# First-layer products of two MLPs over pairs of blocks, halves and chunks (seven products for eight), with softplus in place

## Chip, cores and metric

One core of one Trainium2 chip. The metric is the device time of one execution in microseconds; lower is better. Given are the median of three runs and one profiled execution.

## The reference

Forgetting attention, then two MLPs with 512 model and 2048 hidden columns on 2304 tokens (4 batches, 8 heads, 576 positions, 64 columns a head):

```python
scores = scale * np.matmul(q, k.transpose(0, 1, 3, 2))
decay = cum[:, :, :, None] - cum[:, :, None, :]        # cum: running sum of log f
scores = np.where(causal, -1000000000.0, scores + decay)
...
x = attn_out.transpose(0, 2, 1, 3).reshape(B * S, H * D)
h = x @ w_in1;  g = np.maximum(h, 0.0) + alpha * np.minimum(h, 0.0);  x = g @ w_out1
h = x @ w_in2;  g = np.maximum(h, 0.0) + np.log1p(np.exp(-np.abs(h)));  out = g @ w_out2
```

All is float32 except the MLP weights, which come as float64 (the kernel gets them as 64-bit words).

## The kernel before, in words

**Precision.** Every MLP operand is kept as two parts, a high part (a cast on ScalarE) and a low part (the rest, by a subtraction), and each product is three matmuls: low weight by high data, high by low, high by high. TensorE is PE in the rows, VectorE DVE, ScalarE ACT, GpSimd POOL, and SP issues the DMAs.

**Tiling.** Tokens are cut into 6 chunks of 384 (`CH`), hidden columns into 16 blocks of 128 (`NFF`) in 4 groups of 4 (`G`). `hidden` makes one block for one chunk: 12 matmuls of 384 columns (L889: three part products by four 128-row slices of the model), then the activation. In the first MLP that is two Relu on ScalarE (L896, L899) and a combination on VectorE (L902); in the second VectorE takes −|h| (L911), ScalarE softplus (L915), and VectorE adds max(h, 0) (L918). L925 casts the high part of g, L928 makes the low part. `product` adds four blocks of a group into a bank `o` (L946: 48 matmuls of 384 columns in the first MLP for a chunk's four outputs, of 512 in the second for three), `total` adds that to an accumulator (L965 for the first group, L967), and makes the parts of the second MLP's input (L975, L978) or stores (L982).

**Weights.** `weights` loads a block's raw words and turns them into two parts: on ScalarE L394 and L413, on VectorE L397, L401, L405, L409, L416 and L420. For the first MLP the parts are also stored to DRAM (`w_d`) and loaded again for a second use (L372).

**Stages.** 16 pairs of heads make attention (lines L508 to L804), the first eight with nearly all memory to themselves. Then `switch1` gives half of attention's extra memory to the MLP, and the first MLP for chunks 0 to 2 (`NA` = 3) runs as filler between the attention products of the last eight pairs. Attention rows of the last two batches go to DRAM split into parts (`xb_d`, L811, L814) and are fetched after attention (`fetch`, L849). `switch2` then hands out the rest of the memory, and the first MLP for chunks 3 to 5 and the whole second MLP follow.

**What sets the order.** `Plan` collects every operation with its engine, a length, what it reads and writes, and a rank; `emit` plays it through as a list schedule over buffer slots and writes out each engine's instructions in the order found. The ranks are built from the numbers in `TUNE`. On the chip each engine then works its list strictly in that order.

## Time and profile before

| | us |
|---|---|
| median of 3 runs (1036.82 to 1041.52) | 1039.47 |
| span of the profiled execution, first to last instruction | 1035.1 |
| TensorE busy in it | 1022.3 |
| VectorE busy | 725.1 |
| ScalarE busy | 518.5 |
| GpSimd busy | 240.3 |

The time of the profiled execution as a whole isn't recorded apart from its span; the median lies 4.4 us above the span. Matmuls are pipelined, so a matmul's duration in a row is longer than the step from one to the next, and a busy TensorE isn't by itself TensorE at its peak. Idle time of an engine that nothing waits for costs nothing.

### The profile page before, as it was taken

The page shows a single profiled execution, that of the slowest core. Times are in us where ns is not written, and L with a number is a line of the kernel's source. Part 1 is how long each engine was busy: PE and PEld are TensorE (multiplying, and loading weights), DVE is VectorE, ACT ScalarE, POOL GpSimd, SP SyncE. Part 2 cuts the span into 40 slices and gives each one's busy share as a digit, 9 for nine tenths or more (in the row PEclk, how much of TensorE's full clock was granted, in tenths as well). Part 3 has the DMA queues.
Part 4 walks back from the last instruction along what each step waited for, and adds up shares of the span by engine and source line. Part 5 has one row for each costly group of instructions (what it writes and reads, how often), then busy time and mean ns, then how long its engine had stood idle before and what let it go on. Part 6 is the DMA issues. An engine that isn't in the chain of part 4 may idle for free.

```text
span 1035.1 us, 17156 instructions
## 1 busy us (share of the span) xinstructions
PE 1022.3 (99%) x6023; PEld 946.4 (91%) x6023; DVE 725.1 (70%) x1605; ACT 518.5 (50%) x1264; POOL 240.3 (23%) x399
## 2 busy tenths in 40 slices
PE   8899999999999999999999999999999999999998
PEld 6678899999999899999999999999999998999997
DVE  5898789979999988532335488738765885685543
ACT  6778777776767655344333354434522332332221
POOL 7677766355566520000000000000000000000000
PEclk8999999999999999999999999999999999999999
DMA  7676446646654248020412221202110211010102
GB/s 185 158 225 176 106 124 198 196 147 184 198 167 144 92 159 288 18 71 32 142 40 84 82 61 34 69 1 82 39 45 1 82 41 42 1 41 1 61 31 91
DMA packets 114021, 101.94 MB, mean 98 GB/s; under 512 B 66624, under 2 KB 87248, under 8 KB 113936
## 3 DMA queue, kind: packets, MB, share of 16 engines
q1 hardware_dynamic: 113936, 100.86, 32.3%
q8 instruction: 47, 0.77, 0.3%
q14 instruction: 38, 0.31, 0.1%
HBM read 78.66 MB, written 22.17 MB: 97 GB/s over the span
## 4 chain that ended last, share of the span: by engine, by line
PE 81%; DVE 7%; ACT 4%; issue 3%; POOL 3%; DMA 2%; POOLq 0%; ACTq 0%; DVEq 0%; SPq 0%
PE o L946 36%; PE h L889 35%; PE pt L725 3%; PE pt L621 3%; PE pt L660 2%; POOL d L599 2%; ACT p L651 1%; PE pt L508 1%; DVE d L643 1%; DMA raw<-in_moe_w_in_dram 1%; PE pt L634 1%; DVE p01l L685 1%; DVE ca L409 1%; DVE g L928 1%; DVE acc L967 1%
## 5 line engine op out<-in xcount | busy, mean ns | idle before, releaser
L946 PE MATMUL o<-g,wout 128*128 128x384 f32 x1152 | 213.6, 337 | 0.0
L946 PE MATMUL o<-wout,g 128*128 128x512 f32 x864 | 205.2, 391 | 0.0
L946 PEld LDWEIGHTS o<-g,wout 128*128 128x128 f32 x1152 | 199.4, 188 | 2.3 <-issue 1.9
L946 PEld LDWEIGHTS o<-wout,g 128*128 128x128 f32 x864 | 161.5, 188 | 32.0
L925 ACT CAST g<-h 128x384 fp32r<-128x384 f32 x192 | 92.2, 481 | 141.4 <-PE o L946 126.7
L928 DVE TENSOR_TENSOR g<-h,g 128x384 fp32r<-128x384 f32 x192 | 106.2, 554 | 80.6 <-ACT g L925 79.8
L599 POOL TENSOR_SCALAR d<-cumb,cumc 64x576 f32<-64x576 f32 (+4 forms) x160 | 117.8, 740 | 96.2 <-ACT p L651 90.9
L915 ACT ACTIVATE ta<-ta 128x384 f32<-128x384 f32 x96 | 50.4, 525 | 135.5 <-DVE ta L911 135.2
L902 DVE SCALAR_TENSOR_TENSOR h<-ta,slope,h 128x384 f32<-128x384 f32 x96 | 58.9, 613 | 73.6 <-ACT h L899 73.4
L651 ACT ACTIVATE p<-d,mx 128x128 f32<-128x128 f32 (+2 forms) x144 | 84.4, 588 | 25.8 <-DVE mx L643 24.8
L896 ACT ACTIVATE ta<-h 128x384 f32<-128x384 f32 x96 | 47.3, 492 | 95.2 <-PE h L889 94.6
L911 DVE TENSOR_SCALAR ta<-h 128x384 uint32<-128x384 uint32 x96 | 53.3, 555 | 39.5 <-PE h L889 39.5
L918 DVE SCALAR_TENSOR_TENSOR h<-h,ta 128x384 f32<-128x384 f32 x96 | 54.2, 564 | 38.1 <-ACT ta L915 37.9
L643 DVE CUSTOM_DVE_ANT_0 d<-pt,d 128x128 f32<-128x128 f32 (+2 forms) x144 | 65.3, 477 | 9.7 <-PE pt L626 4.6
L967 DVE TENSOR_TENSOR acc<-o,acc 128x512 f32<-128x512 f32 (+1 forms) x102 | 60.3, 621 | 16.8 <-PE o L946 16.6
L660 PE MATMUL pt<-ident,p 128*128 128x128 f32 (+1 forms) x400 | 65.1, 281 | 4.7 <-ACT p L651 4.3
L660 PEld LDWEIGHTS pt<-ident,p 128*128 128x128 f32 (+1 forms) x400 | 45.7, 140 | 12.3 <-ACT p L651 7.8
L889 PE MATMUL h<-x1h,win 128*128 128x384 f32 x256 | 54.8, 339 | 0.9 <-DVE g L928 0.9
L889 PE MATMUL h<-x2h,win 128*128 128x384 f32 x256 | 55.3, 340 | 0.1
L394 ACT ACTIVATE ca<-raw 128x512 f32<-128x512 f32 x64 | 43.1, 675 | 24.3 <-DMA raw<-in_moe_w_in_dram 11.6
L889 PE MATMUL h<-x0h,win 128*128 128x384 f32 x256 | 54.9, 339 | 0.3 <-DVE g L928 0.3
L889 PE MATMUL h<-x5h,win 128*128 128x384 f32 x256 | 53.5, 335 | 0.0
(157 smaller groups left out, 1909.8 us busy)
## 6 DMA issues: line engine op xcount, KB each, us to landing
raw<-in_moe_w_in_dram SPq DMA_DIRECT2D x32, 512.0 KB, 3.7
raw<-in_moe_w_out_dram SPq DMA_DIRECT2D x32, 512.0 KB, 3.7
cumb<-cum_d SPq DMA_DIRECT2D x30, 288.0 KB, 4.5
out_dram<-acc SPq DMA_DIRECT2D x18, 256.0 KB, 2.1
...
```

The source lines that it names most:

```text
L599: nc.gpsimd.tensor_scalar(out=buf(dk)[r, 0:w], in0=buf(cb)[r, hh, 0:w], scalar1=-1.0, scalar2=cumc[r, e, i:i + 1], op0=ALU.mult, op1=ALU.add,)
L643: nc.vector.tensor_tensor_reduce(out=d[:, c0:c1], in0=buf(key)[:, 0:c1 - c0], in1=d[:, c0:c1], scale=-1.0, scalar=least, op0=ALU.add, op1= ...
L651: nc.scalar.activation(out=buf(pk)[:, 0:w], in_=buf(dk)[:, 0:w], func=AF.Exp, bias=buf(mk)[:, x:x + 1], scale=-1.0, accum_out=buf(sm)[:, e ...
L660: nc.tensor.transpose(out=buf(tk[x])[0:rows, (j - j0) * 128:(j - j0) * 128 + 128], in_=buf(pk)[:, j * 128:j * 128 + rows], identity=ident,)
L889: nc.tensor.matmul(out=hb(), lhsT=w_[:, kk * 128:kk * 128 + 128], rhs=x_[:, kk, :], start=(s == 0), stop=(s == len(ops) - 1))
L902: nc.vector.scalar_tensor_tensor(out=hb(), in0=buf(ka), scalar=slope[:, ff:ff + 1], in1=hb(), op0=ALU.mult, op1=ALU.add)
L911: nc.vector.tensor_scalar(out=buf(ka).bitcast(U32), in0=hb().bitcast(U32), scalar1=0x80000000, scalar2=None, op0=ALU.bitwise_or)
L918: nc.vector.scalar_tensor_tensor(out=hb(), in0=hb(), scalar=0.0, in1=buf(ka), op0=ALU.max, op1=ALU.add)
L925: nc.scalar.copy(out=buf(kg)[0], in_=hb())
L928: nc.vector.tensor_sub(buf(kg)[1], hb(), buf(kg)[0].bitcast(F32))
L946: nc.tensor.matmul(out=buf(ok)[:, 0:width], lhsT=a, rhs=b_, start=(j == 0 and s == 0), stop=(j == G - 1 and s == 2))
L967: nc.vector.tensor_add(buf(ok)[:, 0:width] if inner else ac(), buf(ok)[:, 0:width], ac())
```

## The change

Only chunks 0 and 1 (`NA` = 2) keep the old way beside attention. The other work is cut into five sweeps (`SWEEPS`): first MLP for chunk pairs (2, 3) and (4, 5), second MLP for all three pairs. In a sweep eight half-steps (`inner`) each take two hidden blocks by two chunks, with the 512 model columns in two halves. That is a 2-by-2 product of 2-by-2, and it is made by Strassen's seven products in Winograd's form (`FORM`) instead of eight: 42 matmuls (L1095) instead of 48. The products need sums of weight blocks (`first_weights`: 4 sums and 7 low parts on L1023, GpSimd except for the first two half-steps; 7 casts on L1043, ScalarE) and sums of chunks and halves (`sources`: 4 subtractions on L983, 7 casts on L990, 7 low parts on L993; VectorE for the first sweep, GpSimd for 3 low parts and the subtractions of the others). Their results are put together in PSUM: a copy on ScalarE (L1108) and five additions on VectorE (L1103) a half-step, before the activation (`bend`). `outer` makes the second products as before, now for each output over a whole group (L902).

Softplus is taken in place in PSUM (L862), without the two VectorE operations around it. A weight's float64 words are first put together to float32 (L391, L395, L399) and then split (L412, L415); the second MLP's are prepared in the first two sweeps (`second_weights`). First-layer weights are stored whole, second-layer weights in parts (`w1_d`, `w2_d`), and each sweep loads them again (L1028, L1069). Attention rows of chunks 2 to 5 go to DRAM whole (`xf_d`, L823) and come back by L963; the first MLP's result goes through DRAM for all chunks (`x1_d`). A third switch gives the early MLP's memory to the sweeps. The numbers in `TUNE` are new.

```diff
-    NA = NC // 2
+    NA = 2
...
-            nc.scalar.mul(out=buf(ua), in_=parts()[1], mul=2.0 ** -112)
+            nc.scalar.activation(out=buf(key), in_=halves()[1], func=AF.Prelu, scale=2.0 ** -112, alpha=-(2.0 ** 32))
...
+            w = buf(key).bitcast(U32)
+            nc.vector.tensor_scalar(out=w, in0=w, scalar1=3, scalar2=None, op0=ALU.logical_shift_left)
...
+        def fill():
+            w = buf(key).bitcast(U32)
+            nc.vector.scalar_tensor_tensor(out=w, in0=halves()[0], scalar=29, in1=w, op0=ALU.logical_shift_right,
+                                           op1=ALU.bitwise_or)
...
+            if c < NA:
+                plan.add("act", t_act(n), hi, reads=[yk], writes=[("X", c, hp, b)], rank=R(n0))
+                plan.add("pool", t_pool2(n), lo, reads=[yk], writes=[("X", c, hp, b)], rank=R(n0))
+            else:
+                plan.add("sp", 0.5, put, reads=[yk], writes=[("xf", c, hp, b)], rank=R(n0), late=0.5)
...
+            def soft():
+                nc.scalar.activation(out=hb(), in_=hb(), func=AF.Softplus)
+            plan.add("act", t_act(CH, sbuf=False), soft, writes=[hk], rank=rank)
...
+    PAIRS = tuple((2 * x, 2 * x + 1) for x in range(NC // 2))
+    SWEEPS = ((0, 1), (0, 2), (1, 0), (1, 1), (1, 2))
+    HALVES = NFF // 2
+    PERIOD = 15.6
...
+    FORM = ((0, 0, 1), (4, 4, 2), (5, 5, 3), (3, 3, 4), (1, 1, 1), (6, 2, 4), (2, 6, 5))
...
+        step = PERIOD / 7 * PACE
+        side = "dve" if s == 0 else "pool"
+        both(0, b11, k11, "dve", first)
+        sub(b11, b12, b11, k11, k12, k11, side, first)
+        sub(tf, b22, b11, tk, k22, k11, side, first + step)
+        both(4, tf, tk, "dve", first + step)
+        sub(b12, b22, b12, k12, k22, k12, side, first + 2 * step)
+        both(5, b12, k12, "dve", first + 2 * step)
+        both(3, b11, k11, "dve", first + 3 * step)
+        both(1, b21, k21, side, first + 4 * step)
+        both(2, b22, k22, side, first + 5 * step)
+        sub(b21, tf, b21, k21, tk, k21, side, first + 6 * step)
+        both(6, b21, k21, side, first + 6 * step)
...
+        side = "dve" if s == 0 and a < 2 else "pool"
...
+        both(0, a11, [src[0]], rank)
+        sum_(0, s1, a21, a22, False, [src[1]])
+        sum_(1, s2, s1, a11, True, [src[0], ("sum", s, a, 0)])
+        both(4, s2, [sk, ("sum", s, a, 1)], rank)
+        sum_(2, s3, a11, a21, True, src)
+        both(5, s3, [sk, ("sum", s, a, 2)], rank)
+        both(3, s1, [sk, ("sum", s, a, 0)], rank)
+        both(1, a12, [src[0]], rank)
+        sum_(3, s4, a12, s2, True, [src[0], ("sum", s, a, 1)])
+        both(6, s4, [sk, ("sum", s, a, 3)], rank)
+        both(2, a22, [src[1]], rank)
...
+        def mult(x):
+            wa, xb, n = FORM[x]
+            wkey, xkey = ("ws", s, a, wa), ("xo", s, xb)
+            def pe():
+                w, (xh, xl) = buf(wkey), buf(xkey)
+                done = n in (1, 4) and first[n] == x
+                ops = [(w[:, c], x_, kk) for c, x_ in ((1, xh), (0, xl), (0, xh)) for kk in range(2)]
+                for i, (w_, x_, kk) in enumerate(ops):
+                    nc.tensor.matmul(out=hb(n), lhsT=w_[:, kk * 128:kk * 128 + 128], rhs=x_[:, kk, :],
+                                     start=(i == 0 and first[n] == x), stop=(i == 5),
+                                     skip_group_check=n in (1, 4))
...
+        mult(0)
+        plan.add("act", t_act(CH, sbuf=False), lambda: nc.scalar.copy(out=buf(p1), in_=hb(1)), reads=[bank[1]], writes=[p1],
+                 rank=at[0])
+        mult(1)
+        add(t[1], h[2], t[0], u2, [bank[2], p1], at[1])
+        mult(2)
+        add(t[2], h[3], t[1], u3, [bank[3], u2], at[2])
+        mult(3)
+        add(h[3], h[4], t[2], bank[3], [bank[4], u3], at[3])
+        mult(4)
+        mult(5)
+        add(h[4], h[4], t[1], bank[4], [u2], at[5])
+        mult(6)
+        add(h[5], t[2], h[5], bank[5], [u3], at[6], True)
+        for n, x, ci, k in ((3, 1, 1, 3), (1, 0, 0, 4), (4, 0, 1, 5), (5, 1, 0, 6)):
+            bend(m, 2 * a + x, bank[n], ("g", s, 2 * a + x, ci), at[k])
...
+            slots(pool, "xo", range(1, 7), [128, 2, CH], F32R, 2)
+            slots(pool, "ws", range(1, 8), [128, 2, 256], F32R)
+            slots(pool, "sf", [0], [128, 4, 256])
+            slots(pool, "g", [7], [128, CH], F32R, 2)
+            slots(pool, "w32", [3], [128, 512])
+            slots(pool, "t", range(4), [128, CH])
+            slots(ps, "h", range(2, 5), [128, 512])
+            slots(ps, "o", [2], [128, 512])
...
+                    first_weights(s, a)
+                    if s < 2:
+                        for kind, ff in spare[2 * (s * HALVES + a):2 * (s * HALVES + a) + 2]:
+                            second_weights(kind, ff, T(s, a))
+                    if a % 2 == 0:
+                        for ff in range(2 * a, 2 * a + 4):
+                            last_weights(s, ff, T(s, a + 1) - 4 * PACE)
+                    inner(s, a)
+                if a >= 2 or s > 0:
+                    s0, g = (s, a // 2 - 1) if a >= 2 else (s - 1, NG - 1)
+                    ne = KD if SWEEPS[s0][0] == 0 else CH // 128
+                    for e in range(ne):
+                        outer(s0, g, a % 2, e, T(s, a + (e + 0.5) / ne))
```

How the instructions move, at three places.

TensorE in the first MLP after attention, before: one block `h` for chunk 4, four model slices at a time, then the next block (`win` are the weight parts, 1 low, 0 high).

```order
L889 MATMUL h_0_1998<-x4h,win_1_100 128x384 x4
L889 MATMUL h_0_1998<-x4l,win_0_99 128x384 x4
L889 MATMUL h_0_1998<-x4h,win_0_99 128x384 x4
L889 MATMUL h_0_4991<-x4h,win_1_92 128x384 x4
L889 MATMUL h_0_4991<-x4l,win_0_91 128x384 x4
L889 MATMUL h_0_4991<-x4h,win_0_91 128x384 x4
```

The same engine now, in the first sweep: products of summed weights `ws` and summed sources `xo` (0 high, 1 low), two slices at a time.

```order
L1095 MATMUL h_0_4704<-xo_0_2009,ws_0_4694 128x384 x2
L1095 MATMUL h_0_4704<-xo_1_2010,ws_0_4694 128x384 x2
L1095 MATMUL h_0_4704<-xo_0_2009,ws_0_4694 128x384 x2
L1095 MATMUL h_0_2012<-xo_0_4677,ws_0_4695 128x384 x2
L1095 MATMUL h_0_2012<-xo_1_4678,ws_0_4695 128x384 x2
L1095 MATMUL h_0_2012<-xo_0_4677,ws_0_4695 128x384 x2
L1095 MATMUL h_0_2013<-xo_0_4679,ws_0_4886 128x384 x2
L1095 MATMUL h_0_2013<-xo_1_4680,ws_0_4886 128x384 x2
L1095 MATMUL h_0_2013<-xo_0_4679,ws_0_4886 128x384 x2
```

A block for one chunk had 12 matmuls of its own; now a bank `h` takes 6 for each product, and four results come out of seven such products.

VectorE right behind attention's last operation, before: accumulations and the finishing of early blocks (`acc`, `g`).

```order
L967 TENSOR_TENSOR acc_1982<-o_0_2000,acc_1982 128x384
L967 TENSOR_TENSOR acc_1982<-o_0_1999,acc_1982 128x384
L967 TENSOR_TENSOR acc_1982<-o_0_2000,acc_1982 128x384
L928 TENSOR_TENSOR g_1_1988<-h_0_1997,g_0_1987 128x384
L416 TENSOR_SCALAR cu_0_90<-cu_0_90 128x512
```

VectorE right behind attention's last operation now: behind three accumulations come weight sums (`sf`), their low parts (`ws`) and the sources' low parts (`xo`), between the early blocks' finishing.

```order
L915 TENSOR_TENSOR acc_103<-o_0_2015,acc_103 128x384
L915 TENSOR_TENSOR acc_103<-o_0_2014,acc_103 128x384
L915 TENSOR_TENSOR acc_103<-o_0_2015,acc_103 128x384
L1023 TENSOR_TENSOR sf_0_4696<-w_0_95 128x256
L1023 TENSOR_TENSOR sf_0_4696<-sf_0_4696,w_0_93 128x256
L993 TENSOR_TENSOR xo_1_4678<-tf_0_2008,xo_0_4677 128x768
L993 TENSOR_TENSOR xo_1_4680<-acc_0_2007,xo_0_4679 128x768
L853 SCALAR_TENSOR_TENSOR h_0_2013<-ta_0_2006,slope,h_0_2013 128x384
L1023 TENSOR_TENSOR ws_0_4689<-sf_0_4696,ws_0_4689 128x256
L1023 TENSOR_TENSOR sf_0_4696<-w_0_93,w_0_95 128x256
L993 TENSOR_TENSOR xo_1_4682<-acc_0_2007,xo_0_4681 128x768
L870 TENSOR_TENSOR g_1_1998<-h_0_2013,g_0_1997 128x384
```

The preparation of the first sweep was moved here, ahead of the first additions that its products wait for.

TensorE at the end of the program, before: the last block's parts of three outputs `o` in turn, so that all three banks end together.

```order
L946 MATMUL o_0_4994<-wout_1_1977,g_0_1993 128x512
L946 MATMUL o_0_4994<-wout_0_1976,g_1_1994 128x512
L946 MATMUL o_0_4994<-wout_0_1976,g_0_1993 128x512
L946 MATMUL o_0_1999<-wout_1_1977,g_0_1993 128x512
L946 MATMUL o_0_1999<-wout_0_1976,g_1_1994 128x512
L946 MATMUL o_0_1999<-wout_0_1976,g_0_1993 128x512
L946 MATMUL o_0_2000<-wout_1_1977,g_0_1993 128x512
L946 MATMUL o_0_2000<-wout_0_1976,g_1_1994 128x512
L946 MATMUL o_0_2000<-wout_0_1976,g_0_1993 128x512
```

TensorE at the end now: the last of the seven products, and behind it the first of six outputs, over four blocks; the last block `g_0_1991` comes from that product.

```order
L1095 MATMUL h_0_4704<-xo_0_4881,ws_0_4691 128x384 x2
L1095 MATMUL h_0_4704<-xo_1_4882,ws_0_4691 128x384 x2
L1095 MATMUL h_0_4704<-xo_0_4881,ws_0_4691 128x384 x2
L902 MATMUL o_0_2015<-wout_1_1982,g_0_4697 128x512
L902 MATMUL o_0_2015<-wout_0_1981,g_1_4698 128x512
L902 MATMUL o_0_2015<-wout_0_1981,g_0_4697 128x512
...
L902 MATMUL o_0_2015<-wout_1_1986,g_0_1991 128x512
L902 MATMUL o_0_2015<-wout_0_1985,g_1_1992 128x512
L902 MATMUL o_0_2015<-wout_0_1985,g_0_1991 128x512
```

Each output is now finished before the next begins, and the first one's last three matmuls need the block that was made last.

## Rows read from the trace of the kernel before

**Rows 1.** Page, part 1: busy us (share of the span) and instructions.
```profile
PE 1022.3 (99%) x6023; PEld 946.4 (91%) x6023; DVE 725.1 (70%) x1605; ACT 518.5 (50%) x1264; POOL 240.3 (23%) x399
```

**Rows 2.** Busy time by stretches (us): total, busy (count) by engine, clock, DMA, GB/s.
```profile
0.00:5.00 5.00, 3.59 (x17) 3.60 (x18) 3.17 (x10) 1.97 (x2) 3.87 (x19) 1.00 0.44 101
9.00:15.00 6.00, 4.96 (x23) 3.38 (x23) 1.61 (x8) 2.46 (x10) 4.95 (x10) 0.50 0.74 199
137.00:260.00 123.00, 121.90 (x793) 114.27 (x793) 111.91 (x264) 91.44 (x239) 68.48 (x111) 1.00 0.60 177
260.00:379.00 119.00, 117.86 (x775) 109.47 (x774) 113.01 (x269) 84.85 (x220) 66.59 (x103) 1.00 0.48 148
379.00:1030.00 651.00, 650.90 (x3474) 615.19 (x3473) 389.65 (x741) 240.95 (x493) 2.86 (x2) 1.00 0.19 61
500.00:600.00 100.00, 100.00 (x579) 100.00 (x578) 44.05 (x84) 34.32 (x77) 0.00 (x0) 1.00 0.24 75
```

**Rows 3.** Chain that ended last, by line: from 379 us, then 260 to 379 us.
```profile
by line: PE o L946 48.7%; PE h L889 47.7%; DMA raw<-in_moe_w_in_dram 0.7%; DVE acc L967 0.6%; DVE g L928 0.3%; DVE ta L911 0.2%; DVE cu L401 0.2%; DVE ca L409 0.2%; DVE cu L416 0.2%; DVE h L918 0.1%; issue 0.1%; DVE cu L397 0.1%; DVE wout L
...
by line: PE h L889 15.5%; PE o L946 14.5%; issue 13.6%; POOL d L599 9.7%; PE pt L725 6.0%; PE pt L621 5.0%; PE pt L660 4.5%; DMA cumb<-cum_d 3.9%; POOL d L609 3.6%; DVE p01l L685 2.3%; DVE d L643 2.1%; DVE cu L401 1.7%; POOL v L579 1.6%; DV
```

**Rows 4.** Line L725 from 375 us: count, ns min/median/max, first and last start.
```profile
L725 PE MATMUL pt<-p01l,v x10: 274/307/309, 375.9 to 378.2; 128*128 128x320 f32 x6, 128*128 128x192 f32 x2, 128*128 128x64 f32 x2
```

**Rows 5.** GpSimd groups by shape: busy us, mean ns | idle before.
```profile
L834 POOL TENSOR_TENSOR x1l<-x,x1h 128x192 fp32r<-128x192 f32 x8 | 4.7, 593 | 1.6 <-ACT x1h L831 1.5
...
L834 POOL TENSOR_TENSOR x2l<-x,x2h 128x384 fp32r<-128x384 f32 x4 | 4.0, 1008 | 0.0
```

**Rows 6.** VectorE groups by shape, same columns.
```profile
L928 DVE TENSOR_TENSOR g<-h,g 128x384 fp32r<-128x384 f32 x192 | 106.2, 554 | 80.6 <-ACT g L925 79.8
...
L902 DVE SCALAR_TENSOR_TENSOR h<-ta,slope,h 128x384 f32<-128x384 f32 x96 | 58.9, 613 | 73.6 <-ACT h L899 73.4
...
L409 DVE SCALAR_TENSOR_TENSOR ca<-ca,raw 128x512 f32<-128x512 uint32 x64 | 46.9, 734 | 0.6
...
L401 DVE SCALAR_TENSOR_TENSOR cu<-raw,cu 128x512 uint32<-128x512 uint32 x64 | 44.7, 698 | 0.5
...
L405 DVE TENSOR_SCALAR ca<-raw 128x512 uint32<-128x512 uint32 x64 | 30.8, 481 | 0.1
...
L397 DVE TENSOR_SCALAR cu<-ca 128x512 uint32<-128x512 uint32 x64 | 28.9, 456 | 4.0 <-ACT ca L394 3.6
...
L416 DVE TENSOR_SCALAR cu<-cu 128x512 uint32<-128x512 uint32 x64 | 28.1, 439 | 4.2 <-ACT win L413 3.7
...
L420 DVE SCALAR_TENSOR_TENSOR wout<-ca,cu 128x512 fp32r<-128x512 f32 x32 | 22.3, 699 | 0.5
...
L685 DVE TENSOR_TENSOR p00l<-pt,p00h 128x256 fp32r<-128x256 f32 x24 | 9.8, 416 | 3.3 <-ACT p00h L681 3.0
```

**Rows 7.** ScalarE groups by shape, same columns.
```profile
L925 ACT CAST g<-h 128x384 fp32r<-128x384 f32 x192 | 92.2, 481 | 141.4 <-PE o L946 126.7 <-DVE h L902 12.3 <-PE h L889 1.0
```

**Rows 8.** DMA issues (median us to landing), and the rate in 40 slices.
```profile
wout<-w_dh SPq DMA_DIRECT2D x12, 256.0 KB, 2.5
...
GB/s 185 158 225 176 106 124 198 196 147 184 198 167 144 92 159 288 18 71 32 142 40 84 82 61 34 69 1 82 39 45 1 82 41 42 1 41 1 61 31 91
```

**Rows 9.** Instructions in order of time at the end: start us, us, what.
```profile
1020.65 10.59 PE L946 MATMUL o<-wout,g 128*128 128x512 f32 x46
...
1029.92 2.05 DVE L967 TENSOR_TENSOR acc<-o,acc 128x512 f32<-128x512 f32 x3 [6.11 <-PE o L946]
```

**Rows 10.** Lines L409, L928 in 150:375 (GpSimd working), then 400:1030 (idle).
```profile
L409 DVE SCALAR_TENSOR_TENSOR ca<-ca,raw x23: 673/690/1753, 152.2 to 370.9; 128x512 f32<-128x512 uint32 x23
...
L928 DVE TENSOR_TENSOR g<-h,g x35: 535/551/560, 151.5 to 373.0; 128x384 fp32r<-128x384 f32 x35
...
L409 DVE SCALAR_TENSOR_TENSOR ca<-ca,raw x32: 681/686/698, 400.1 to 921.4; 128x512 f32<-128x512 uint32 x32
...
L928 DVE TENSOR_TENSOR g<-h,g x150: 547/557/561, 408.2 to 1019.6; 128x384 fp32r<-128x384 f32 x150
```

More of the change, by code (lines that the diff above doesn't have):

```diff
@@ L76, in add, with touch @@
         return n
+    def touch(self, n, key):
+        deps = self.ops[n][3]
+        deps.update(x for x in self.writers.get(key, ()) if x != n)
+        self.readers.setdefault(key, []).append(n)
     def everything(self):
@@ L359, in forgetting_attention_two_mlps, with raw_weights, halves @@
     PT = []
[L362 to L378 removed]
+    def raw_weights(m, kind, ff, rank):
+        key = ("w32", "raw", m, kind, ff)
+        rkey = ("raw", key)
+        def halves():
             words = buf(rkey).bitcast(U32).rearrange("p (n two) -> p n two", two=2)
[L380 to L381 removed]
+            return words[:, :, 0], words[:, :, 1].bitcast(F32)
         def load():
@@ L431, in weights @@
-        plan.add("dve", t_dve(512), low, reads=[ua, uu], writes=[key], rank=rank, port=True)
-        if m == 0:
-            kept.add((kind, ff))
-            if ff < NFF - G:
-                def save():
-                    for a in range(2):
-                        nc.sync.dma_start(out=w_d[a][kind, ff], in_=buf(key)[a].bitcast(F32))
-                plan.add("sp", 1.3, save, reads=[key], writes=[saved], rank=rank, late=2.92)
+            w = buf(key).bitcast(U32)
+            nc.vector.tensor_scalar(out=w, in0=w, scalar1=3, scalar2=None, op0=ALU.logical_shift_left)
@@ new lines, in keep, with save, early_weights @@
+    def keep(m, kind, ff, key, rank):
+        def save():
+            if kind == 0:
+                nc.sync.dma_start(out=w1_d[m][ff], in_=buf(key))
+            else:
+                for a in range(2):
+                    nc.sync.dma_start(out=w2_d[m][ff, :, a], in_=buf(key)[a].bitcast(F32))
+        plan.add("sp", 0.65 * (1 + kind), save, reads=[key], writes=[("wd", m, kind, ff)], rank=rank, late=0.73 * (1 + kind))
+    def early_weights(kind, ff, key, rank):
+        src = raw_weights(0, kind, ff, rank)
+        if kind == 0:
+            keep(0, 0, ff, src, rank)
+        split(key, src, "dve", rank)
+        if kind == 1:
+            keep(0, 1, ff, key, rank)
@@ L990, in output @@
[L990 to L1002 removed]
+                nc.vector.tensor_add(acc(), buf(ok)[:, 0:width], acc())
```

411 lines of the change are left out of this document (219 added, 192 removed), and 3 rows, old and new, of the table TUNE.

## The prediction

> **What bounds the kernel now.** I read the engines' totals first, then the busy time by stretches, then the chain of waits. TensorE is busy for 99% of the span [rows 1], but a busy share doesn't say where it is at its peak, so look at the stretches [rows 2]. From 379 us to 1030 us TensorE is busy 650.9 of 651 us at granted clock 1.00, VectorE 389.7, ScalarE 241, GpSimd 3. There the chain of waits is all products: 48.7% on L946 and 47.7% on L889 [rows 3]. So after attention only fewer or shorter matmuls help. What one costs is its cadence, not its duration in the table, which overlaps the next: 579 matmuls of 384 columns in 500 to 600 us make 172.7 ns each. The order lists 3480 matmuls after attention, 864 of them with 512 columns; (651 − 2616 × 0.1727) / 864 = 230 ns for one of those. Attention's last product starts at 378.2 us [rows 4]. Before that TensorE is still busy 121.9 of 123 and 117.9 of 119 us, but here VectorE is nearly full too (111.9 and 113.0), and the chain from 260 us on names GpSimd, issue and DMA beside TensorE [rows 2, 3]: a mixed stage.
>
> **Matmuls removed: −41.4 us.** In the five sweeps (chunk pairs 1 and 2 of the first MLP, all three of the second) one half-step makes two blocks for two chunks. Before, that was 2 × 2 × 12 = 48 matmuls; now seven products of 6, 42. Five sweeps of 8 half-steps save 240, and the order agrees: 384 + 1680 first-product matmuls where there were 2304; L902 issues the same 2016 as L946 did. 240 × 0.1727 = 41.4 us, on the path, since TensorE had 0.1 us idle there. The shapes (128x128 by 384) don't change, so I keep the cadence.
>
> **What pays for it.** A half-step with its share of second products takes TensorE (42 + 48) × 0.1727 = 15.5 us (second MLP: 42 × 0.1727 + 36 × 0.230, also 15.5). Beside it stand, all new:
> - GpSimd: 4 sums and 7 low parts of 256 columns. The nearest rows are 192 columns 0.593 us and 384 columns 1.008 [rows 5]; on their line 256 costs 0.73 and 768 costs 1.83. So 11 × 0.73 = 8.0, plus 7 source operations of 768 in a sweep, 12.8 / 8 = 1.6: 9.6 of 15.5 us.
> - VectorE: 5 recombining additions at 0.554, 4 low parts at 0.554, in the first MLP 4 × 0.613 and about 3 accumulations; 9.1 us. In the first two sweeps the second MLP's raw weights come too, 2 × (0.456 + 0.698) + 0.699 = 3.0 [rows 6]. 12.1 of 15.5; in the second MLP some 6.5.
> - ScalarE: at most 7 + 1 + 12 operations below 0.5 us [rows 7], 10 us, and two raw-weight operations.
>
> None reaches 15.5, so I cost them at nothing; the cover is TensorE's own half-step, and an engine that went over it would cost the excess 40 times. The in-place softplus takes two VectorE operations per block off (about 0.55 each, 96 blocks), where VectorE was no bound: zero.
>
> On the engine for the sums the trace and a rule pull apart. GpSimd's 1.008 us for 384 columns is 1.8 times VectorE's 0.554 [rows 5, 6]. The Trainium skill (GPSIMD Engine Reference, 4.1 Engine selection) says to keep elementwise work on VectorE, since GpSimd is about 2 times slower with two inputs; the ratio agrees. By that rule the 11 operations would cost VectorE 11 × 0.416 = 4.6, and 12.1 + 4.6 = 16.7 would pass 15.5: some 19 us lost over 16 half-steps. What counts by the rows is which engine has room, and GpSimd was empty, so the sum stays.
>
> **The queues.** SP issues 657 rows instead of 385. Four second-layer blocks serve a group; with six buffers two of the next are there early, and two (four transfers of 256 KB, 1.05 MB) wait for the old group's last product. TensorE meanwhile has 36 first products, 6.2 us. A landing took 2.5 us and a slice moved 288 GB/s [rows 8], so 2.5 + 1.05 MB / 288 = 6.1 us as an upper bound, and the first six matmuls of the group need only the early blocks: zero, at worst 1 us at 19 changes. SP also waits for GpSimd to give back the first-weight buffers, and second-layer loads stand behind that; GpSimd's 38% slack covers it.
>
> **Transition: +5.9 us.** When attention ends, VectorE still has to make the first sweep's sources and the weights of two half-steps, since all of that is placed there. In its order, from the third accumulation behind attention to the addition that the sixth product waits for (row h_0_4705<-h_0_4706,t_0_4702), stand 19 operations of 256 columns (0.416), 5 of 768 (0.554 and 0.699 for 384 and 512, so 0.99), 4 accumulations and 9 others: 20.2 us [rows 6]. They start 6.8 us after attention, when the third second product (36 × 0.1727) has been added, and end at 27.0. TensorE has 138 matmuls until there, 23.8 us: 3.2 late. Ten products on, the same count gives 39.8 against 34.2, and after the last source 48.4 against 42.5. I take 5.9, since it is a count of this very order. The low end is 0, should VectorE get this work done before attention ends; the high end 12, should the hand-overs from ScalarE, which the count leaves out, add as much again.
>
> **Attention: −1 us.** The new weight route costs VectorE 0.456 + 0.698 + 0.699 = 1.85 us a block instead of the six operations' 3.52 [rows 6]; 33 against 30 blocks before attention ends, and fewer activations: about 49 us less VectorE. GpSimd and ScalarE lose the splitting of the last eight pairs' rows. TensorE's visible idle there is only 2.2 us [rows 2]. The order puts 672 early MLP matmuls ahead of the last attention product, not 840, so I expect it at about 378 − 168 × 0.1727 = 349 us. Gain at most 2.2; I take 1.
>
> **The end: −0.6 us.** Before, three 512-column additions stood behind the last matmul (2.05 us) [rows 9]; now one (0.68): −1.4. New is that the last product's addition, softplus, cast and low part (some 0.55 + 0.5 + 0.48 + 0.554, with hand-overs 2.9) lie under nine matmuls (2.07): +0.8.
>
> **Sum.** 1035.1 − 41.4 + 5.9 − 1 − 0.6 = 998 us span. The median of the runs shown, 1039.5, is 4.4 above the profiled span, which I keep: **1002 us**, 3.6% faster.
>
> **Rivals.**
> 1. *Attention doesn't shorten.* It loses a third of its filler, and if its own chain (GpSimd 13.3%, issue 13.6% and DMA 3.9% from 260 us on [rows 3]) sets its pace, it still ends at 378 and all 29 us of moved work stand behind: 998 + 29 + 4.4 = 1031, still over 0.5% faster. Against it: 96 early matmuls remain in the order when attention ends, so filler never runs out. 0.07.
> 2. *A bank hand-over shows once in each half-step.* Seven products share five banks; if one reuse waits for a cast and a low part (0.481 + 0.554 [rows 6, 7]) 40 times, 41 us come back: 1043, no change. The point is whether a bank's finishing chain (some 4 us) is longer than the products between: there are 36 to 72 matmuls (6 to 12 us) in the order. 0.04.
> 3. *GpSimd and VectorE shut each other out; slower.* The place is the first two sweeps. If every VectorE operation waited while GpSimd works, a half-step needs 12.1 + 8.0 = 20.1 us; it decides from 15.5 on, and 16 × 4.6 = 74 us are lost: 1076. For it: a VectorE operation on two SBUF inputs took up to 1753 ns beside GpSimd, median 690, but never over 698 with GpSimd idle [rows 10]. Against it: the cast's low part, with one input in PSUM, has 551 and 557 ns with and without GpSimd; most of the new VectorE work is of that kind. The Trainium skill (SBUF — State Buffer, SBUF: two separate sides) calls the shared port pair an exclusive lock, taken by VectorE only in a two-port mode or with two SBUF inputs. By that rule 3.0 + 9.6 us share the pair in a half-step and no time is lost; the trace agrees as far as these two rows go. 0.03.
>
> TensorE's clock: it was granted 0.50 (1.2 GHz instead of 2.4) from 9 to 15 us, after TensorE had worked 3.6 of the first 5 us [rows 2]. Should the transition's gaps bring that back for as long, 6 us of work at half speed add 3 us; within the range. That the change doesn't cut the matmuls is excluded by the order.
>
> **Chances.** Forecast 0.86; rivals 0.07, 0.04, 0.03. A change under 0.5% (5 us) is about what a measurement of this kernel can't tell from none. Forecast and rival 1 are faster: 0.93; rival 2 same, 0.04; rival 3 slower, 0.03. Range: downward transition 0 and the full 2.2 of attention give 995, and 2 for the runs' own spread; upward transition 12 (+6), a quarter of rival 1 (+7) and some group changes at up to 1 us: 1016.
>
> **What would show it.** Right: 42 products in 7.25 us and half-steps of 15.5 us with TensorE over 99%; attention's last product near 349 us; a gap of some 6 us within 45 us behind it, its releaser VectorE L1103 or L1023; GpSimd near 60% in the sweeps. Wrong: TensorE waits that recur each half-step (releaser GpSimd L1023: rival 3 or GpSimd short; VectorE L870: rival 2); an attention end beyond 360 us.

## The result, and the profile after

The changed kernel takes 1013.2 us (median of 4 runs, 1010.8 to 1014.0), the kernel before 1038.1 on the same chip: a ratio of 0.976, 95% interval 0.974 to 0.978. The forecast was 1002 us with a range of 993 to 1016: the sign was right, the gain is 25 us instead of 37, and the time lies in the upper part of the range. The profiled span is 1009.0 us where the sum gave 998.0, so 11 us are to be explained. The median stands 4.2 us above the span, where 4.4 was forecast, but that agreement is partly luck: the profiled run itself took 1010.8 us, 1.8 more than its span, and was the shortest of the four.

The page's first part, beside [rows 1]:

```profile
PE 986.7 (98%) x5783; PEld 906.5 (90%) x5783; DVE 666.8 (66%) x1430; ACT 615.6 (61%) x1567; POOL 576.7 (57%) x833
```

240 fewer matmuls, GpSimd from 23% to 57%. Where the time went is seen in the stretches (columns as in [rows 2]): the first 130 us, the rest of attention, the transition, the sweeps of the first MLP, and those of the second:

```profile
0.00:130.00 130.00, 120.03 (x877) 94.68 (x878) 95.48 (x295) 94.32 (x288) 87.45 (x166) 0.95 0.62 162
130.00:354.40 224.40, 221.94 (x1499) 205.94 (x1499) 195.36 (x479) 171.02 (x458) 119.19 (x221) 1.00 0.65 194
354.40:449.60 95.20, 88.97 (x496) 86.80 (x495) 76.86 (x140) 60.39 (x144) 44.82 (x51) 0.98 0.71 232
449.60:640.00 190.40, 190.40 (x1100) 190.40 (x1099) 141.12 (x249) 125.73 (x298) 133.28 (x155) 1.00 0.65 218
680.00:960.00 280.00, 280.00 (x1401) 252.86 (x1400) 122.69 (x210) 133.31 (x312) 163.56 (x209) 1.00 0.35 116
```

**The sweeps are as forecast.** TensorE doesn't idle at all in either stretch. 190.4 us / 1100 is 173.1 ns a matmul (172.7 forecast), so a half-step of 90 takes 15.6 us; in the second MLP 78 of 1401 make 15.6 us too (15.5 forecast). In it VectorE works 141.12 / 190.4 × 15.6 = 11.6 us (12.1 forecast) and 6.8 (6.5), GpSimd 10.9 and 9.1 (9.6), ScalarE 10.3 in the first MLP (at most 10, and two raw-weight operations). From 440 us on the chain of waits is products alone:

```profile
by line: PE o L902 54.3%; PE h L1095 45.1%; DVE acc L915 0.1%; issue 0.0%
```

**Attention ended late.** Its last product starts at 354.4 us; 378.2 [rows 4] less 168 matmuls (29.0) and 1 us would have been 348.2.

**The transition was long.** From attention's last product to 449.68 us the order has 492 matmuls, 85.0 us at 0.1727; they took 95.2. So 10.2 us were lost, 5.9 forecast. TensorE's waits from 350 to 1000 us (line waited for: total us, times, longest):

```profile
PE h L1095 <- ACT xo L990: 2.2, 1, 2.2
PE h L1095 <- DVE h L1103: 2.0, 1, 2.0
PE h L1095 <- POOL ws L1023: 0.9, 2, 0.6
PE h L1095 <- ACT t L1108: 0.5, 1, 0.5
PE h L1095 <- DVE g L870: 0.5, 1, 0.5
PE h L885 <- DVE g L870: 0.2, 1, 0.2
```

The longest is one the forecast didn't have. In order of time, on four engines (start us, us, what, [idle before <-releaser]):

```profile
354.77 0.42 ACT L758 COPY xt<-pt 64x320 f32<-64x320 f32 x1 [0.17 <-PE pt L727]
356.83 1.43 POOL L806 TENSOR_TENSOR x<-x,rb 128x576 f32<-128x576 f32 x1 [12.46 <-DMA rb<-rd]
358.28 0.81 SPq L823 DMA_DIRECT2D xf_d<-x  x2
362.52 0.84 ACT L990 CAST xo<-tf 128x768 fp32r<-128x768 f32 x1 [7.33 <-DMA wout<-w_d]
366.35 1.89 PE L1095 MATMUL h<-xo,ws 128*128 128x384 f32 x6 [2.20 <-ACT xo L990]
```

The sums for the sources had long been made (309 us for `tf`), yet ScalarE's cast of them waits 7.3 us. Its output `xo` lies in memory that `switch2` takes over from attention, and attention isn't through when TensorE is: its last tile is still to be multiplied (356.8) and stored (358.3). The profile names a transfer that landed at the same moment (`wout<-w_d`, whose tile isn't read by that cast). After the gap TensorE was granted half its clock (0.50, 1.2 GHz, from 367 to 370 us; 0.60 over 366 to 370), and 13 matmuls went where 23 fit at 172.7 ns.

```profile
362.00:366.00 4.00, 2.14 (x13) 1.82 (x11) 3.40 (x6) 3.48 (x7) 0.00 (x0) 1.00 0.85 252
366.00:370.00 4.00, 3.65 (x13) 3.69 (x14) 4.00 (x10) 3.84 (x10) 0.00 (x0) 0.60 0.01 2
```

Up to 377.4 us this costs 4.2 us. Another 2.6 us go between 377 and 409 us, in waits of at most 0.5 us each (for ScalarE's copy, VectorE's low part and GpSimd's low part). The second large loss, 3.3 us between 409 and 432, has the second MLP's raw weights in it (engines in order of time):

```profile
416.20 2.29 POOL L983 TENSOR_TENSOR acc<-acc 128x768 f32<-128x768 f32 x1
416.71 2.06 DVE L395 TENSOR_SCALAR w<-w 128x512 uint32<-128x512 uint32 x1
418.81 1.11 DVE L399 SCALAR_TENSOR_TENSOR w<-raw,w 128x512 uint32<-128x512 uint32 x1
419.94 0.32 SPq L424 DMA_DIRECT2D w_d<-w  x1
422.21 0.67 ACT L391 ACTIVATE w<-raw 128x512 f32<-128x512 f32 x1 [4.20 <-DMA w_d<-w]
425.73 2.38 PE L1095 MATMUL h<-xo,ws 128*128 128x384 f32 x12 [1.99 <-DVE h L1103]
```

VectorE's shift takes 2.06 us beside GpSimd's 2.29 us subtraction (0.456 for the nearest operation in [rows 6], 0.42 in the middle here). By the order of events the store and with it ScalarE wait for it, and casts and recombining additions stand behind in their queues; whether this conversion is the cause is tried below.

### The profile page after: what moved, and what is told of

Read it like the earlier page. It is cut to its first block, busy times and chain, and to the rows that moved or that the text cites. A ratio compares the mean times of both kernels' runs of the same rounds, so it can differ in the third digit from the quotient of the medians.

```text
span 1009.0 us, 18030 instructions
## 1 busy us (share of the span) xinstructions
PE 986.7 (98%) x5783; PEld 906.5 (90%) x5783; DVE 666.8 (66%) x1430; ACT 615.6 (61%) x1567; POOL 576.7 (57%) x833
## 4 chain that ended last, share of the span: by engine, by line
PE 74%; DMA 3%; ACT 1%; issue 1%; DVE 1%; POOL 1%; SPq 0%; ACTq 0%; DVEq 0%; POOLq 0%
PE o L902 37%; PE h L1095 27%; PE h L885 5%; PE pt L727 2%; PE pt L662 2%; PE pt L623 1%; DMA raw<-in_moe_w_in_dram 1%; PE pt L510 1%; DMA w_d<-wout 1%; DMA w<-w_d 0%; PE pt L636 0%; POOL ws L1023 0%; POOL sf L1023 0%; DMA wout<-w_d 0%; ACT xo L990 0%
## 5 line engine op out<-in xcount | busy, mean ns | idle before, releaser
L1095 PE MATMUL h<-xo,ws 128*128 128x384 f32 x1680 | 311.3, 336 | 6.2 <-ACT xo L990 2.2
L1095 PEld LDWEIGHTS h<-xo,ws 128*128 128x128 f32 x1680 | 294.9, 188 | 12.6 <-POOL ws L1023 2.8
L902 PE MATMUL o<-g,wout 128*128 128x384 f32 x1152 | 214.7, 338 | 0.0
L902 PE MATMUL o<-wout,g 128*128 128x512 f32 x864 | 207.3, 392 | 0.0
L1023 POOL TENSOR_TENSOR ws<-sf,ws 128x256 fp32r<-128x256 f32 x152 | 118.2, 784 | 148.8 <-ACT ws L1043 146.6
L902 PEld LDWEIGHTS o<-g,wout 128*128 128x128 f32 x1152 | 200.8, 189 | 1.7 <-issue 1.2
L902 PEld LDWEIGHTS o<-wout,g 128*128 128x128 f32 x864 | 161.4, 188 | 32.0 <-ACT g L867 0.4
L870 DVE TENSOR_TENSOR g<-h,g 128x384 fp32r<-128x384 f32 x192 | 104.3, 552 | 84.4 <-ACT g L867 83.6
L915 DVE TENSOR_TENSOR acc<-o,acc 128x384 f32<-128x384 f32 (+1 forms) x126 | 77.0, 612 | 78.6 <-PE o L902 77.6
L1043 ACT CAST ws<-sf 128x256 fp32r<-128x256 f32 x160 | 63.3, 407 | 102.0 <-PE h L1095 62.9
L1023 POOL TENSOR_TENSOR ws<-w,ws 128x256 fp32r<-128x256 f32 x114 | 88.2, 774 | 44.4 <-ACT ws L1043 41.0
L645 DVE CUSTOM_DVE_ANT_0 d<-pt,d 128x128 f32<-128x128 f32 (+3 forms) x144 | 66.1, 479 | 17.8 <-POOL d L601 6.7
L1043 ACT CAST ws<-w 128x256 fp32r<-128x256 f32 x120 | 48.6, 407 | 47.9 <-PE h L1095 37.3
L862 ACT ACTIVATE h<-h 128x384 f32<-128x384 f32 x96 | 45.1, 475 | 51.4 <-DVE h L1103 31.5
L1103 DVE TENSOR_TENSOR h<-h,t 128x384 f32<-128x384 f32 x80 | 45.0, 562 | 46.3 <-PE h L1095 45.8
L391 ACT ACTIVATE w<-raw 128x512 f32<-128x512 f32 x64 | 43.2, 678 | 23.0 <-DMA raw<-in_moe_w_in_dram 9.5
```

The source lines that it names most:

```text
L645: nc.vector.tensor_tensor_reduce(out=d[:, c0:c1], in0=buf(key)[:, 0:c1 - c0], in1=d[:, c0:c1], scale=-1.0, scalar=least, op0=ALU.add, op1= ...
L870: nc.vector.tensor_sub(buf(kg)[1], hb(), buf(kg)[0].bitcast(F32))
L902: nc.tensor.matmul(out=buf(ok)[:, 0:width], lhsT=a, rhs=b_, start=(j == 0 and s == 0), stop=(j == last and s == 2))
L915: nc.vector.tensor_add(acc(), buf(ok)[:, 0:width], acc())
L1023: getattr(nc.vector if side == "dve" else nc.gpsimd, fn)(*args)
L1043: nc.scalar.copy(out=buf(key)[:, 0], in_=get())
```

## Experiments

Kernels are compared by their ratios to the kernel before, run beside them on the same chip (some 1038 us, so 0.001 is 1 us). "Loss" is the time from attention's last product to the last matmul, less the matmuls there at 0.1727 and 0.230 us: 2.4 us before, 12.7 after the change. It is read from one profile of each kernel, and that of the changed kernel is the shortest of its four runs by 2.2 us, so differences of the loss of 1 to 3 us are rough.

### What a matmul is worth, both ways

```diff
-                for i, (w_, x_, kk) in enumerate(ops):
+                for again in range(2 if x == 1 else 1):
+                    for i, (w_, x_, kk) in enumerate(ops):
...
```

> The second of the seven products is issued twice in each of the 40 half-steps (its bank is started anew, so the result is the same): 6 more matmuls a half-step, nothing else is moved. If TensorE's stream is all that bounds the sweeps, all 240 lie on the path: 240 x 0.1727 = +41.4 us on the changed kernel's 1013.2, 1054.6, and the stretch from 440 to 1000 us stays full. If another engine bounds a part of the half-steps (GpSimd is busy up to 17.8 of 20 us in some stretches), the added matmuls fall into its waits: at most half, +20 us, 1033.

1047.6 us, ratio 1.011 (1.009 to 1.013); the span grows by 36.8 us, TensorE is busy 40.00 of 40 us in every stretch from 440 to 1000. Attention ends 1.4 us earlier in this profile and the loss is 9.4 instead of 12.7 us: the added matmuls give the transition's late work 3.3 us. (36.8 + 1.4 + 3.3 = 41.5 proves nothing by itself, as the loss is counted with 0.1727 us a matmul.) The price is seen behind the transition. From one and the same second-layer product on (L902, started at 451.8 us in the changed kernel and at 453.1 here), the time to the last matmul is 553.2 and 588.6 us, with 204 of the added matmuls in it: 173.7 ns each, their full cadence. So the 240 removed matmuls were worth 41 to 42 us in the sweeps; by the ratios of the whole they were worth 36, since part was given back in the transition.

```diff
-                for i, (w_, x_, kk) in enumerate(ops):
+                for i, (w_, x_, kk) in enumerate(ops[5:] if x == 1 else ops):
...
-                                     start=(i == 0 and first[n] == x), stop=(i == 5),
+                                     start=(i == 0 and first[n] == x), stop=(x == 1 or i == 5),
```

> Left out: five of the six matmuls of the second product in each half-step, 200 in all; every other instruction stays. If nothing is near TensorE as a bound, 200 x 0.1727 = -34.5 us: 978.7. If GpSimd (11 operations of 256 columns at 0.78 us and 1.6 us for sources, 10.2 us of a half-step that would be 14.7 us long) or VectorE in the first two sweeps (12.1 us by the prediction's count) runs in chains with the casts that don't overlap, waits recur in each half-step and less than 20 us is gained: 993 or more.

988.9 us, ratio 0.954 (0.951 to 0.957): 24 us gained of 34.5, between the two. The loss rises by 12.0 us. About half of that is in the transition: up to 460 us the loss is 16.4 us, 10.3 in the changed kernel. The rest is in the first MLP's sweeps, which now wait too, with a granted clock of 0.96 in one stretch; the second MLP's don't. The next bound is near in the first two sweeps only:

```profile
520.00:560.00 40.00, 37.46 (x206) 36.61 (x205) 28.12 (x50) 28.43 (x69) 25.17 (x27) 0.96 0.80 272
680.00:720.00 40.00, 40.00 (x199) 35.84 (x198) 20.61 (x33) 19.75 (x47) 22.53 (x30) 1.00 0.28 86
```

### The engine for the sums

```diff
-        side = "dve" if s == 0 and a < 2 else "pool"
+        side = "dve"
```

> The weight sums and low parts of all half-steps go from GpSimd to VectorE (in the changed kernel only the first sweep's first two half-steps have them there). By the prediction's count VectorE then needs 12.1 + 11 x 0.416 = 16.7 us in a half-step of 15.5 in the first two sweeps: 16 x 1.2 = +19 us, 1032, with TensorE waiting for VectorE there and not in the last three sweeps (6.5 + 4.6 = 11.1 us). Rival: VectorE's count is too high, as each operation on two tiles is shorter with GpSimd idle: no change, 1013. Second rival: VectorE and GpSimd stood in each other's way in the changed kernel, and the transition gets shorter: 1008.

1026.6 us, ratio 0.988 (0.984 to 0.992): 12 to 13 us lost (19 expected), in the transition and the first two sweeps, none in the last three. In the two profiles, where attention ends 1.6 us earlier than in the changed kernel, the loss rises by 17.2 us. One stretch of each kind:

```profile
480.00:520.00 40.00, 36.81 (x202) 36.17 (x201) 35.70 (x73) 21.87 (x50) 7.55 (x4) 0.96 0.68 221
720.00:760.00 40.00, 40.00 (x205) 36.52 (x204) 31.77 (x66) 20.89 (x49) 7.69 (x4) 1.00 0.41 136
```

VectorE is busy 35.7 of 40 us there: not over its time, as the forecast of 16.7 us in 15.5 had it, but waited for. It gets part of the added work back, as its operations on two tiles in SBUF are shorter with GpSimd nearly idle. From 440 to 640 us (by shape: busy us, mean ns), changed kernel first:

```profile
L399 DVE SCALAR_TENSOR_TENSOR w<-raw,w 128x512 uint32<-128x512 uint32 x21 | 17.6, 851 | 0.2
L415 DVE TENSOR_TENSOR wout<-w,wout 128x512 fp32r<-128x512 f32 x11 | 11.0, 1021 | 0.0
L870 DVE TENSOR_TENSOR g<-h,g 128x384 fp32r<-128x384 f32 x50 | 26.9, 551 | 5.4 <-ACT g L867 5.1
```

```profile
L399 DVE SCALAR_TENSOR_TENSOR w<-raw,w 128x512 uint32<-128x512 uint32 x22 | 16.5, 760 | 0.0
L415 DVE TENSOR_TENSOR wout<-w,wout 128x512 fp32r<-128x512 f32 x11 | 7.5, 685 | 0.6 <-ACT wout L412 0.6
L870 DVE TENSOR_TENSOR g<-h,g 128x384 fp32r<-128x384 f32 x49 | 26.6, 551 | 3.5 <-ACT g L867 3.2
```

L870, with an input in PSUM, takes 551 ns in both. The Trainium skill (SBUF — State Buffer, SBUF: two separate sides) lets VectorE and GpSimd shut each other out only when VectorE reads two operands from SBUF or runs in a two-port mode; these rows agree. L395, with one operand in SBUF, also takes 522 ns in the changed kernel and 420 here; by that rule it would run in a two-port mode, which no row shows. The rule of the Trainium skill to keep such work on VectorE (GPSIMD Engine Reference, 4.1 Engine selection) would cost 12 to 13 us here, so the measurement decides against it for this kernel.

### The memory that attention hands over

```diff
-        slots(sb, "x32", ids("x32", 1, 1), [128, S])
+        if extra:
+            slots(sb, "x32", ids("x32", 1, 1), [128, S])
...
-        slots(sb, "rb", [0], [128, S])
...
         slots(left, "w32", range(3), [128, 512])
+        slots(left, "x32", [0], [128, S])
+        slots(left, "rb", [0], [128, S])
```

> The tiles x32 (number 0) and rb of attention are kept in memory that no later tile takes over; the order of every engine is the same. Theory: TensorE's first gap behind attention (2.2 us idle from 364.1 us, then matmuls at half clock, 4.2 us in all from 354.5 to 377.4 us) comes from the sources' casts, which wait until the last attention tile has been multiplied, stored and landed (362.4 us), because they are written into its memory. Then the casts start at about 355 us and 3.5 to 4.2 us go: 1009 to 1010. Rival, the prediction's: VectorE's queue of work behind attention sets the gap, whatever the memory: under 1 us gained, 1012.5 or more, with the first gap's releaser VectorE.

1007.0 us, ratio 0.971 (0.969 to 0.973). The cast starts at 352.6 us, 1.5 us after attention's last product instead of 8.1, the gap shrinks from 2.2 to 1.35 us, and the clock stays at 1.00:

```profile
352.61 0.84 ACT L990 CAST xo<-tf 128x768 fp32r<-128x768 f32 x1 [0.67 <-DMA rb<-rd]
...
362.24 1.28 PE L1095 MATMUL h<-xo,ws 128*128 128x384 f32 x6 [1.35 <-DMA w<-w_d]
```

The first 108 matmuls behind attention take 20.4 us instead of 22.8. So the theory holds for the cast and the gap behind it, but it brings 2.4 us there, not 3.5 to 4.2: by the profile the load of weights (`w<-w_d`) is late next. The rest of the 5 us by ratio isn't owed to it with certainty: the loss falls by only 1.2 us, and this profile's attention ended 3.2 us earlier, with every engine's order the same.

### Softplus as it was

```diff
+            def minus():
+                nc.vector.tensor_scalar(out=buf(ka).bitcast(U32), in0=hb().bitcast(U32), scalar1=0x80000000, scalar2=None,
+                                        op0=ALU.bitwise_or)
...
-                nc.scalar.activation(out=hb(), in_=hb(), func=AF.Softplus)
+                nc.scalar.activation(out=buf(ka), in_=buf(ka), func=AF.Softplus)
...
+            def whole():
+                nc.vector.scalar_tensor_tensor(out=hb(), in0=hb(), scalar=0.0, in1=buf(ka), op0=ALU.max, op1=ALU.add)
...
```

> The second MLP's softplus goes back to its old form beside the product's bank: two VectorE operations of 384 columns more for each of 192 half blocks (the changed kernel's bend runs on every pair of a 128-row block and a chunk), some 0.5 us each. The prediction put the in-place form at zero: VectorE is busy 0.44 of the time in the second MLP and would go to about 0.7. Then 1013, within 2 us. Rival: the extra step lengthens the chain that gives a bank back, and TensorE waits a little in each of 24 half-steps: 0.5 us each, +12 us, 1025.

1009.4 us, ratio 0.973 (0.971 to 0.975): no slower than the changed kernel, though VectorE rises to 0.7 of the second MLP. (There are 96 such half blocks, not 192.) The in-place form is worth nothing here.

```profile
680.00:720.00 40.00, 40.00 (x198) 35.76 (x198) 28.22 (x52) 16.36 (x39) 20.24 (x29) 1.00 0.30 97
```

### Raw weights later

```diff
-                    if s < 2:
-                        for kind, ff in spare[2 * (s * HALVES + a):2 * (s * HALVES + a) + 2]:
+                    if s < 3:
+                        for kind, ff in spare[slice(0, 2) if s + a == 0 else slice(max(2, 2 * (s * HALVES + a - 3)), max(2, 2 * (s * HALVES + a - 2)))]:
```

> The conversion of the second MLP's raw weights starts 3 half-steps later (after one half-step's share it pauses until the fifth, and ends in the third sweep). Theory: the transition's last gap (3.3 us between 409 and 432 us: ScalarE waits 4.2 us for a buffer whose store waits for VectorE's conversion, 2.06 us for an operation that takes 0.42 with GpSimd idle, and the recombining additions stand behind it) comes from this conversion, and some of the 2.6 us between 377 and 409. Then 3 to 5 us go: 1008 to 1010. Rival: the gap is VectorE's and GpSimd's backlog from the sources and weight sums, which does not change: within 1.5 us of 1013. Second rival: the conversion only moves its gaps to half-steps 5 to 19: 1013.

1007.5 us, ratio 0.972 (0.970 to 0.973), 4.7 us less than the changed kernel. Of that, 2.0 us are attention's earlier end in this profile, with TensorE's order the same up to there. The gap at 425 us is gone: from 387.5 to 438 us TensorE doesn't wait. A part comes back later (39.28 and 39.49 of 40 us busy from 440 to 520), so the loss falls from 12.7 to 10.9. The first gap stays, and behind it a granted clock of 0.68 over 365 to 369 us. TensorE's waits from 350 to 1000 us:

```profile
PE h L1095 <- ACT xo L990: 2.4, 1, 2.4
PE h L1095 <- DVE h L1103: 1.1, 1, 1.1
PE h L1095 <- ACT t L1108: 0.7, 1, 0.7
PE h L1095 <- DVE g L870: 0.2, 1, 0.2
```

### The first half of attention

Two kernels with one edit each: the constants of `TUNE` for the first eight pairs (`TILE1` and the first number of each pair) are exchanged between the kernels.

> The order's constants for the first eight attention pairs are those of the kernel before (the second half's and everything else as changed). Looked at: when the eighth pair's row sums are stored, 129.1 us in the kernel before, 131.2 to 134.2 us in five profiles of the changed order. Theory: the changed constants cost 2 to 5 us there: 129 us, whatever comes later. Rival: the constants do not matter and the start's own spread does it: 131 to 134 us. The end may be later, since the later order is not fitted to it.

> The kernel before, with the changed kernel's constants for the first eight attention pairs. By the same theory the eighth pair's row sums are stored 2 to 5 us later than the 129.1 us of the kernel before: 131 to 134 us; by the rival 129 us within 1.

The eighth pair's sums are stored at 130.1 us in the changed kernel with the old constants, at 128.9 in the old kernel with the new ones. So neither expectation of the constants is met in both: by this mark the constants do nothing in the old code, and in the new code the old ones bring most of the delay back (131.2 to 134.2 there with the new ones). TensorE's busy time in the first 130 us, looked at afterwards, goes with the code instead. In order: the kernel before, the kernel before with new constants, the changed kernel with old ones:

```profile
0.00:130.00 130.00, 123.36 (x928) 100.56 (x929) 104.40 (x317) 97.23 (x301) 97.23 (x174) 0.96 0.63 169
```

```profile
0.00:130.00 130.00, 123.45 (x914) 97.57 (x915) 104.01 (x312) 96.05 (x295) 93.14 (x171) 0.96 0.64 167
```

```profile
0.00:130.00 130.00, 121.26 (x903) 95.04 (x904) 97.52 (x299) 96.76 (x297) 87.22 (x170) 0.97 0.62 165
```

Eleven profiles of the changed attention (this kernel and its variants) have 117.3 to 121.2. With one profile of each mixture this points to the code and doesn't settle it, and what in the code does it (the weights' route, two chunks for three, the buffers) wasn't tried. As whole kernels neither mixture is of use: the changed kernel with old constants took 1034.0 us in its one run, its attention's last product at 374.9 us, and the old kernel with new ones 1044.7, at 381.8. The later order was not made for them; what delays it wasn't taken apart.

### Both mends together

> The edits of e4 and e6 together. If the two gaps are separate, as the theory has it (the first waits for attention's last store, the later ones for the conversion), their gains add: e4 ran at 0.9711 and e6 at 0.9715 of the kernel before, the changed kernel at 0.976, so 0.9666 of the kernel before, some 1003 us. If both only give room to the same backlog on VectorE, the second edit gains nothing more: 0.971, 1007 us.

1005.5 us, ratio 0.967 (0.964 to 0.969), as expected if the two gaps are separate: the gains add, and this version beats both kernels. The loss is 8.7 us.

### How much room GpSimd has

```diff
+            def twice():
+                for _ in range(2 if side == "pool" else 1):
+                    two("tensor_sub" if minus else "tensor_add", out(), x(), y())
...
```

> Every weight sum on GpSimd is computed twice (the result is the same), in the order of the changed kernel: 4 more operations of some 0.78 us in each half-step. GpSimd goes from 9.8 us (327.5 us in 520 us, 33.5 half-steps) to 12.9 us of 15.5. Prediction's theory, that GpSimd costs nothing until it fills the half-step: 1013, within 3 us (the transition may grow by 1 or 2). Rival, GpSimd's work stands in a chain with ScalarE's casts and VectorE shares its path: 0.5 us or more in each of 38 half-steps, 1032 or more.

1052.3 us, ratio 1.011 (1.007 to 1.015): 36 us slower than the changed kernel, though GpSimd is busy only 77% of the time from 440 to 680 us (36.0 of 40 us at most). The rival holds, but only in the transition and the first MLP's sweeps:

```profile
480.00:520.00 40.00, 37.39 (x215) 36.75 (x214) 29.88 (x54) 25.32 (x60) 33.96 (x40) 1.00 0.60 200
720.00:760.00 40.00, 40.00 (x199) 35.74 (x198) 17.82 (x32) 17.24 (x43) 30.89 (x43) 1.00 0.30 94
```

In the second MLP (720 to 960 us) GpSimd is busy 30 to 34 of 40 us and TensorE 39.7 or more. In the first sweeps ScalarE's casts wait much longer for GpSimd's sums, while GpSimd's low parts wait less for those casts than before: the wait has moved into ScalarE's queue, where activations and casts of `g` stand behind it. From 440 to 680 us the changed kernel had (us in total, times, longest)

```profile
POOL ws L1023 <- ACT ws L1043: 59.3, 53, 5.3
ACT ws L1043 <- POOL sf L1023: 26.1, 20, 3.0
...
DVE g L870 <- ACT g L867: 13.1, 17, 1.4
```

and with the sums twice (L1046 is the same cast, L1098 the products)

```profile
ACT ws L1046 <- POOL sf L1023: 71.1, 40, 4.6
POOL ws L1023 <- ACT ws L1046: 34.6, 43, 2.7
...
DVE g L870 <- ACT g L867: 21.4, 16, 3.4
...
PEld h L1098 <- POOL ws L1023: 14.8, 9, 4.1
```

The same cast waits 56.4 us for the sums in the second MLP too (720 to 1000 us), and costs TensorE next to nothing there. So the waits alone don't explain the 36 us; in the first sweeps they reach TensorE.

In the next run the same loop also stands around the low parts.

> Sums and low parts on GpSimd are all computed twice (the result is the same): 11 more operations, 9.8 + 8.7 = 18.5 us in a half-step of 15.5. By the prediction's theory GpSimd is the bound then, and the excess of 3.0 us shows in each of 38 half-steps: +114 us, 1127. If it costs much more (over 1160), waits in the chain with ScalarE's casts add to it; if much less (under 1090), GpSimd's operations get shorter when VectorE waits, or the half-steps' spare time is larger than thought.

1198.2 us, ratio 1.152 (1.148 to 1.156): 183 us slower, more than the 114 of GpSimd's excess, and past the 1160 us from which the expectation lets waits add to it. TensorE idles in all sweeps (28.1 to 38.5 of 40 us busy from 440 to 1160), its granted clock at 0.86 to 0.96 there.

The last run is the first of these three with the doubled length in the plan, so that every order is made anew (the line below is against that run):

```diff
-            plan.add(side, took, twice, reads=reads, writes=[sk, ("sum", s, a, n)], rank=rank, port=True)
+            plan.add(side, took * (2 if side == "pool" else 1), twice, reads=reads, writes=[sk, ("sum", s, a, n)], rank=rank, port=True)
```

> As e10 (every weight sum on GpSimd computed twice), but the planner is given the doubled duration, so the order of every engine's queue is made for it. e10 cost 36 us although GpSimd's total stayed below the half-step, all of it in the first two sweeps and the transition, where ScalarE's casts of the sums stood in its queue ahead of the activations that TensorE's banks wait for. If that order is the cause, a new order brings most of it back: 1023 us or less (10 us over the changed kernel). If the work itself does not fit beside VectorE's in the first two sweeps, whatever the order, 1040 to 1050 us remain.

1038.0 us, ratio 0.999 (0.997 to 1.001). A new order brings back 12 of the 36 us; 24 remain, again only up to the end of the first MLP's sweeps. That lies between the two expectations and nearer to the second: a third was the order, and two thirds stay in the one new order that was tried. That the work doesn't fit beside VectorE's is a likely reason, which was not taken apart further. One of GpSimd's own operations is a tenth longer there too, where VectorE works on raw weights (from 440 to 640 us, then from 720 to 960; busy us, mean ns):

```profile
L1023 POOL TENSOR_TENSOR ws<-sf,ws 128x256 fp32r<-128x256 f32 x45 | 37.9, 852 | 24.0 <-ACT ws L1046 24.0
...
L1023 POOL TENSOR_TENSOR ws<-sf,ws 128x256 fp32r<-128x256 f32 x64 | 49.1, 773 | 38.4 <-ACT ws L1046 38.4
```

## Why the prediction was right, and where it wasn't

- **Matmuls removed, −41.4:** right. The cadence held (173.1 ns), TensorE is full in the sweeps, and matmuls put back there cost 173.7 ns each.
- **What pays for it, zero:** right as a result. The counts of a half-step are within 0.5 us for VectorE and 1.3 for GpSimd, ScalarE's stays under its bound, and no wait recurs; rivals 2 and 3 didn't come. But the reason, that no engine's sum reaches 15.5 us, doesn't carry in the first two sweeps: 3.1 us more of GpSimd's work a half-step were not hidden there, though the sum would still have been below 15.5. What had room was the second MLP.
- **The sums on GpSimd:** right against VectorE, which would have cost 12 to 13 us (19 worked out), though by waits for an engine that wasn't full and not by an excess over the half-step.
- **The queues:** zero at the group changes is right: no wait for second-layer weights stands in the list of TensorE's waits above. In the transition a store of raw weights, which ScalarE waited 4.2 us for, stood ahead of the gap at 425 us.
- **Transition, +5.9:** mis-sized, measured 10.2 (4.2, 2.6 and 3.3). VectorE's count was near the truth (the addition forecast at 27.0 us behind attention ran at 30.2), but two things weren't in it. `xo`'s memory is free only when attention's last tile is stored: 4.2 us up to 377.4, of which e4 took away 2.4. And operations of raw weights were costed at their mean in the kernel before, 0.456 us for one that took 2.06 beside GpSimd: 3.3 us around 425, which e6 took away. The 2.6 between them, in small waits, weren't taken apart. The clock's return to 0.50 behind the first gap, put at up to 3 us, is in the 4.2.
- **Attention, −1:** this is the step that failed most, 6.2 us. The second part was right: filler never ran out, and from 130 us on TensorE idled 2.5 us of 224. The first 130 us, which the prediction took as unchanged without a reason ([rows 2] show them only up to 15 us), have TensorE busy 3.3 us less; the two profiles of the old code have 123.4 and 123.5 us, twelve of the new code 117.3 to 121.3, so this goes with the new code rather than with the constants, and its cause there stays open. Of the other 2.9 us, 1.0 is the gain that didn't come, and 1.4 may be the spread of runs: in eleven profiles attention's last product started between 351.2 and 356.1 us, at 353.0 in the middle one. The last 0.5 stay open. Rival 1 didn't come either: 23.8 of the 29.0 us moved out of attention showed.
- **The end, −0.6:** −0.1 measured: 4.1 us from the last matmul's start to the end of the span, 4.2 before. The first two of the three additions in [rows 9] started before the last matmul's end (1031.2 us), so only the last had been on the path; nothing is seen of the +0.8 either.

998.0 + 6.2 + 4.3 + 0.5 = 1009.0: attention, transition and end make up the miss. The range held them because its upper end had room for these very two terms, 12 us of transition and 7 for attention; but the 7 were allowed for a filler that runs short, which it didn't, so that part of the room was luck.
